# Attention, then a cosine MoE layer: raw w_out stores first, transposed probabilities in groups of six and eight, one PSUM copy shared by two engines

## The chip, the cores and the metric

The kernel runs on one core of one Trainium2 chip. The metric is the device time of one execution in microseconds. The profile follows the engines TensorE (PE, its weight loads PEld), VectorE (DVE), ScalarE (ACT), GpSimd (POOL) and SyncE (SP, which here only issues DMAs; a name with q is an engine's instruction queue).

## The reference

```python
# q, k, v: 4 batches, 12 heads, 448 positions, head width 64
scores = q @ k.T / sqrt(64);  scores[above the diagonal] = -1e9
attn = exp(scores - max);  attn = attn / (sum + 1e-9);  y = attn @ v
x = y as 1792 tokens x 768
h = x @ w_in            # 768 x 2048
out = (h * cos(h)) @ w_out   # 2048 x 768
```

The two weight matrices lie in DRAM as 64-bit floats; everything else is 32-bit.

## The kernel before

**Attention.** The work is 24 steps of one batch and two heads (`pairs`, N = 24). A step's rows are cut into seven blocks of 64 queries, and block m has m blocks of 64 keys. The instructions of each engine stand in the order in which the Python code writes them, so each engine is a queue. In step i (lines 596 to 626) PE computes the scores of pair i (`scores`, L391), the product with v of pair i-2 (`av`, L444), transposes q and k of pair i+2 (L341), transposes the probabilities of pair i-1 (`tp`, L424) and the finished output of pair i-2 (`turn_out`, L483). DVE adds the mask, takes each row's minimum and moves the scores from PSUM to SBUF in seven pieces (`masked`, L400), divides the output of pair i-2 (`divide`, L472 to L474), and copies transposed probabilities from PSUM to SBUF (L345). ACT makes the exponentials (L407) and the other copies from PSUM (L347, L502).

**The transposed probabilities.** They come in two groups (`GROUPS`), each for two heads, and each group and head fills one PSUM bank: `evac_tp(i, g, bs, h, dve)` copies one of these four from PSUM into the tile `pm`, on DVE where `dve` is true. Group 0 goes to banks 7 and 4, group 1 to banks 5 and 6. The same banks take the next step's scores: the first piece (m = 4) goes to bank 7, m = 7 to bank 4, m = 5, 1 and 2 to bank 6, m = 6 to bank 5. So the first scores of step i+1 wait for the copy of group 0, head 0, which is always DVE's first copy after the division. The copy of group 1, head 0 is DVE's when i is even and ACT's third when i is odd.

**The first weights.** Between steps, twelve pieces (128 x 256) of the first w_in and w_out tiles are turned into 32-bit floats (`convert_weight`), each piece in two halves. After an even step DVE shifts and masks the upper words (L139, L142); after an odd step it puts in the lower words (L148) and sets numbers below a bound to zero (L152). What POOL has to do for a piece is put into the list `postponed` and run at the start of the next step (`take_postponed`): after the first half the square of the upper word (L145), after the second the rounded high part and the rest (L156, L157). POOL also interleaves the raw q and k (L272) and splits the attention output into a high and a low part (L507, L508). A DMA that SP issues one step later stores the raw w_out piece (`raw_out`, L1427).

**The MoE part.** w_in and w_out are taken in 8 groups of 256 columns of the hidden layer. Every product is three matmuls: high x high, high x low, low x high. Tokens 0 to 1023 come first (`slot`), while DVE and ACT unpack the next weights (`mask`, `pack`), `halve` splits a tile (ACT L769, POOL L770) and POOL issues the DMAs that keep halves and raw w_out in DRAM (`spill_halves`, `spill_raw`). The other 768 tokens follow with seven block products in place of eight, from the tiles kept in DRAM.

Of the kernel before, what the change touches and what calls it, by code (L numbers as in the profile page):

```python
# [10 lines left out]
F32 = mybir.dt.float32  # L11
# [5 lines left out]
ALU = mybir.AluOpType  # L17
# [4 lines left out]
def kernel(  # L22
# [86 lines left out]
    def f32(ap):  # L109
        return ap.bitcast(F32)  # L110
# [20 lines left out]
    def convert_weight(st, w, pool, parts=1, j=0, halves=(0, 1)):  # L131
        n = DM // parts
        wh, wl = (w[:, x, j * n : (j + 1) * n] for x in range(2))
        lo32, hi32 = st[0][:, :, 0], st[0][:, :, 1]
        hif = f32(hi32)
        if 0 in halves:
            t = pool.tile([P, EH], U32, tag="ct", bufs=2, name="ct")[:, 0:n]
            st.append(t)
            nc.vector.tensor_scalar(  # L139
                t, hi32, 3, 0x3FFFFFFF, op0=ALU.logical_shift_left, op1=ALU.bitwise_and  # L140
            )
            nc.vector.scalar_tensor_tensor(  # L142
                t, hi32, 0xC0000000, t, op0=ALU.bitwise_and, op1=ALU.bitwise_or
            )
            return lambda: nc.gpsimd.tensor_tensor(hif, hif, hif, op=ALU.mult), None  # L145
        if 1 in halves:
            t = st[1]
            nc.vector.scalar_tensor_tensor(  # L148
                t, lo32, 29, t, op0=ALU.logical_shift_right, op1=ALU.bitwise_or
            )  # L150
            tf = f32(t)
            nc.vector.scalar_tensor_tensor(tf, hif, W_MIN2, tf, op0=ALU.is_ge, op1=ALU.mult)  # L152


            def rounded():
                nc.gpsimd.tensor_copy(wh, tf)  # L156
                nc.gpsimd.tensor_tensor(wl, tf, f32(wh), op=ALU.subtract)  # L157

            return rounded, tf
# [73 lines left out]
    def attention(filler_of, postponed):  # L233
        with (
# [108 lines left out]
            def evac(dst, src, dve=False):  # L343
                if dve:
                    nc.vector.tensor_copy(dst, src)  # L345
                else:
                    nc.scalar.copy(dst, src)  # L347
# [57 lines left out]
            def exps(i, *ms):  # L405
# [3 lines left out]
                    )  # L409

            GROUPS = [
                [(6, 0), (7, 0), (6, 1), (7, 1), (6, 2), (7, 2), (3, NM)],
                [(2, 0), (4, 0), (3, 0), (5, 0), (4, 1), (5, 1), (5, NM)],
            ]
            spots = {e: (g, x) for g, es in enumerate(GROUPS) for x, e in enumerate(es)}

            def open_ptr(i):
                ptr[i] = at.tile([P, 2, 2, NM, R], F32, tag="pm", bufs=2, name="pm")

            def tp(i, g, bs):  # L420
                for x, (m, kc) in enumerate(GROUPS[g]):
# [5 lines left out]
                        )  # L427

            def evac_tp(i, g, bs, h, dve=False):
                evac(  # L430
                    ptr[i][:, g, h].rearrange("p n r -> p (n r)"),
                    banks8[:, bs[h], 0 : NM * R], dve,
                )

            def obank(i):
                return 4 if i == N - 1 else 0

            def av(i):
                (vn, vo), pt, ob = vals.pop(i), ptr[i], obank(i)

                def add(m, j, y, lhsT, rhs, start=False, stop=False):
                    b, n, h = PLACE[m]
                    c = (2 * n + j) * E1
                    nc.tensor.matmul(  # L444
                        banks8[half(h), ob + b, c : c + E1], lhsT=lhsT, rhs=rhs, start=start, stop=stop
                    )

                for j in range(2):
                    for y in range(2):
                        for a, ms in enumerate(LAST):  # L450
                            m, ys = ms[y], half(y)
                            g, n = spots[ms[0], NM]
                            add(
                                m, j, y, pt[ys, g, j ^ SWAP[m], n],
                                vo[ys, a, i % 2, j] if y else vn[ys, m // 2, j], start=j == 0,
                            )
                pieces = [(7, 6, k) for k in range(3)] + [(5, 4, k) for k in range(2)] + [(2, 3, 0)]
                for x, (ma, mb, k) in enumerate(pieces):
                    for j in range(2):
                        for m in (ma, mb):  # L460
                            g, n = spots[m, k]
                            add(
                                m, j, 0, pt[:, g, j ^ SWAP[m], n], vn[:, k, j],
                                stop=j == 1 and x in (2, 5),
                            )

# [75 lines left out]
            for i in range(N):  # L542
                take_postponed()
                if i == 0:
                    load_raw(3)
                if i:
                    load_v(i)
                if i + 4 < N:
                    load_raw(i + 4)
                open_step(i)  # L550
                if i < 3:
                    scores(i, slice(0, 4))
                    if i < 2:
                        transpose_in(i + 1, TB_)
                    else:
                        tp(0, 1, (0, 1))
                    scores(i, slice(4, 8))
                if i == 0:
                    masked(i, 4, 3)
                    exps(i, 4)  # L560
                    evac_in(1, 0, True)
                    evac_in(1, 1)
                    masked(i, 7, 6, 5, 1, 2)
                    exps(i, 3, 7, 6, 5, 1, 2)
                    interleave(3)
                    yield i
                    continue
                if i == 1:
                    masked(i, 4, 3, 7, 6, 5)
                    evac_in(2, 0)  # L570
                    evac_in(2, 1)
                    exps(i, 4, 3)
                    open_ptr(0)
                    tp(0, 0, (0, 1))
                    evac_out(0, 0, (0, 1), 0)
                    masked(i, 1, 2)
                    exps(i, 7, 6)
                    interleave(4)
                    yield i
                    continue  # L580
                if i == 2:
                    transpose_in(3, TB_)
                    evac_out(0, 1, (0, 1), 0)
                    exps(1, 5, 1, 2)
                    masked(i, 4, 3)
                    exps(i, 4, 3)
                    masked(i, 7, 6)
                    exps(i, 7)
                    evac_in(3, 0, True)
                    evac_in(3, 1)  # L590
                    masked(i, 5, 1, 2)
                    exps(i, 6, 5, 1, 2)
                    av(0)
                    divide(0)
                    transpose_in(4, TB_)
                else:
                    scores(i)
                    if i < N - 1:
                        evac_in(i + 1, 0)
                        evac_in(i + 1, 1)  # L600
                    masked(i, 4, 3, 7, 6, 5, 1, 2)
                    exps(i, 4, 3, 7, 6, 5, 1, 2)
                    av(i - 2)
                    divide(i - 2)
                    if i < N - 2:
                        transpose_in(i + 2, TB_)
                G1, G2 = ((7, 4), (5, 6)) if i < N - 1 else (TB_, (4, 5))
                open_ptr(i - 1)
                tp(i - 1, 0, G1)
                evac_out(i - 1, 0, G1, 0)  # L610
                tp(i - 1, 1, G2)
                evac_tp(i - 1, 1, G2, 1)
                evac_tp(i - 1, 1, G2, 0, i % 2 == 0)
                if i == N - 1:
                    fill(4)
                if i + 3 < N:
                    interleave(i + 3)
                put_out(i - 2)
                if i == N - 1:
                    fill(2)  # L620
                    open_ptr(i)
                    tp(i, 1, (4, 5))
                    evac_out(i, 1, (4, 5), 0)
                    tp(i, 0, TB_)
                    evac_out(i, 0, TB_, 0)
                yield i
# [91 lines left out]
    def moe(ring, early, firsts):  # L718
        pend = None
        with tc.tile_pool(name="mo", bufs=1) as mo:  # L720
# [42 lines left out]
            def halve(i):  # L763
                if i >= len(todo):
                    return
                kind, f = todo[i]
                w = ring[kind, f] = weight_tiles(kind, (wpool, mo)[f // 2 % 2])
                tf = f32(masks.pop((i, 0))[:])
                nc.scalar.copy(w[:, 0], tf)  # L769
                nc.gpsimd.tensor_tensor(w[:, 1], tf, f32(w[:, 0]), op=ALU.subtract)  # L770
                spill_halves(kind, f, w)
                if kind:
                    spill_raw(f, tf)
                return tf

            def sums_tile(pool, tag, bufs, dtype=F32R):
# [714 lines left out]
```

## Time and profile before

| | |
|---|---|
| time, median of 3 runs | 592.44 us (591.93 to 592.61) |
| the profiled execution's own time | 589.68 us |
| its span in the profile | 587.9 us |
| busy share of the span | PE 99%, DVE 77%, ACT 68%, POOL 71% |
| chain that ended last, by engine | PE 81%, DVE 15%, issue 1%, DMA 1% |
| granted TensorE clock, mean | 0.998 |

PE is counted busy where its pipelined matmuls overlap, so its 99% doesn't say that it never waits. The chain that ended last is followed back from the last instruction: it says which engine's work set the end in each stretch. Its DVE share lies in the attention part; behind that it is PE almost alone.

### The profile page before, as it was taken

How to read it: one execution, taken by the hardware profiler on the slowest of the kernel's cores; microseconds unless marked ns; L12 is line 12 of the kernel's file. 1: busy time of each engine (PE TensorE's matmuls, PEld its weight loads, DVE VectorE, ACT ScalarE, POOL GpSimd, SP SyncE). 2: the span in 40 equal slices, each digit the busy share in tenths (PEclk: the TensorE clock that was granted, in tenths of full speed). 3: DMA queues.
4: the chain of work that ended last, by engine and by line, in shares of the span. 5: the costliest groups of instructions: out<-in, count | busy, mean ns of one | idle time of the engine just before them, and what ended most of it. 6: DMA issues, size and time to landing. Idle time of an engine off the chain costs nothing.

```text
span 587.9 us, 15297 instructions
## 1 busy us (share of the span) xinstructions
PE 579.7 (99%) x5895; PEld 538.9 (92%) x5895; DVE 455.2 (77%) x953; ACT 401.7 (68%) x788; POOL 419.6 (71%) x448
## 2 busy tenths in 40 slices
PE   9999999999999999999999999999999999999996
PEld 6888888888899999999999999999999999999996
DVE  5999999995767878778778767743587787787786
ACT  5999999997667777878777777532454554564540
POOL 2466666755377887977787877915678978978894
PEclk9999999999999999999999999999999999999999
DMA  9976676665268597876868796599987746748105
GB/s 182 211 175 156 163 177 156 167 178 184 80 216 299 171 337 257 300 273 210 303 197 313 218 337 225 229 354 401 378 293 246 255 160 231 263 164 284 43 1 161
DMA packets 92409, 131.55 MB, mean 224 GB/s; under 512 B 35024, under 2 KB 77216, under 8 KB 92336
## 3 DMA queue, kind: packets, MB, share of 16 engines
q1 hardware_dynamic: 84832, 106.52, 58.3%
q0 software_dynamic: 4736, 22.42, 9.9%
q10 hardware_dynamic: 2768, 1.64, 1.0%
q8 instruction: 46, 0.75, 0.5%
q14 instruction: 27, 0.22, 0.1%
HBM read 83.36 MB, written 47.19 MB: 222 GB/s over the span
## 4 chain that ended last, share of the span: by engine, by line
PE 81%; DVE 15%; DMA 1%; issue 1%; POOL 0%; ACTq 0%; DVEq 0%
PE banks L746 23%; PE banks L1175 13%; PE banks L1195 13%; PE banks L651 8%; PE banks L650 7%; PE banks L652 7%; DVE pb L400 7%; DVE pm L345 3%; PE banks L391 3%; DVE on L474 2%; PE banks L1212 2%; PE banks L1099 2%; PE banks L444 2%; DMA vn<-in_v_dram 1%; DVE ct L142 1%
## 5 line engine op out<-in xcount | busy, mean ns | idle before, releaser
L734 DVE TENSOR_TENSOR acc<-acc,banks 128x768 f32<-128x768 f32 (+1 forms) x122 | 112.7, 932 | 42.9 <-PE banks L746 32.6
L746 PE MATMUL banks<-w,gh 128*128 128x384 f32 x512 | 109.7, 335 | 0.0
L746 PEld LDWEIGHTS banks<-w,gh 128*128 128x128 f32 x512 | 90.9, 188 | 1.3 <-DVE acc L734 0.2
L651 PE MATMUL banks<-xa,w 128*128 128x512 f32 x192 | 75.2, 392 | 0.0
L652 PE MATMUL banks<-xa,w 128*128 128x512 f32 x192 | 75.0, 391 | 0.0
L650 PE MATMUL banks<-xa,w 128*128 128x512 f32 x192 | 74.9, 390 | 0.0
L407 ACT ACTIVATE pb<-pb,stat 128x256 f32<-128x256 f32 (+6 forms) x168 | 71.5, 527 | 2.6 <-DVE stat L400 2.6
L746 PE MATMUL banks<-w,gl 128*128 128x384 f32 x256 | 65.1, 335 | 0.0
L770 POOL TENSOR_TENSOR w<-ct,w 128x768 fp32r<-128x768 f32 x28 | 52.4, 1872 | 15.1 <-ACT w L769 9.1
L400 DVE CUSTOM_DVE_ANT_0 pb<-banks,mask 128x256 f32<-128x256 f32 (+6 forms) x168 | 60.1, 420 | 3.7 <-PE banks L391 3.7
L658 ACT ACTIVATE ni<-banks 128x512 int32<-128x512 f32 (+1 forms) x64 | 34.5, 539 | 33.7 <-PE banks L652 20.2
L677 POOL TENSOR_TENSOR gl<-r,gh 128x512 fp32r<-128x512 f32 x32 | 42.2, 1320 | 15.9 <-ACT gh L676 15.7
L660 DVE SCALAR_TENSOR_TENSOR r<-ni,banks 128x512 f32<-128x512 int32 (+1 forms) x56 | 35.1, 626 | 23.5 <-ACT ni L658 23.0
L662 ACT ACTIVATE r<-r 128x512 f32<-128x512 f32 (+1 forms) x56 | 32.8, 586 | 22.1 <-DVE r L660 21.5
L444 PE MATMUL banks<-vn,pm 128*64 128x65 f32 (+1 forms) x1344 | 47.5, 223 | 0.0
L746 PEld LDWEIGHTS banks<-w,gl 128*128 128x128 f32 x256 | 46.4, 188 | 0.0
L444 PEld LDWEIGHTS banks<-vn,pm 128*64 128x64 f32 (+1 forms) x1344 | 44.2, 137 | 1.8
L665 DVE SCALAR_TENSOR_TENSOR r<-r,banks 128x512 f32<-128x512 f32 (+1 forms) x56 | 35.0, 626 | 13.9 <-ACT r L663 13.9
L391 PE MATMUL banks<-flat 64*64 64x64 f32 (+5 forms) x768 | 43.5, 357 | 1.5 <-DVE pm L345 0.2
L1175 PE MATMUL banks<-xb,bb 128*128 128x384 f32 x234 | 44.7, 334 | 0.0
L652 PEld LDWEIGHTS banks<-xa,w 128*128 128x128 f32 x192 | 36.0, 188 | 7.5
L650 PEld LDWEIGHTS banks<-xa,w 128*128 128x128 f32 x192 | 36.1, 188 | 7.3
(143 smaller groups left out, 1430.5 us busy)
## 6 DMA issues: line engine op xcount, KB each, us to landing
bb<-w_in_d SPq DMA_DIRECT2D x48, 384.0 KB, 5.7
land<-in_moe_w_in_dram SPq DMA_DIRECT2D x14, 768.0 KB, 6.1
land<-in_moe_w_out_dram SPq DMA_DIRECT2D x14, 768.0 KB, 5.6
big<-w_out_d SPq DMA_DIRECT2D x25, 384.0 KB, 5.1
w_out_d<-w POOLq DMA_DIRECT2D x8, 768.0 KB, 5.1
w_in_d<-w POOLq DMA_DIRECT2D x7, 768.0 KB, 4.2
raw_d<-ct POOLq DMA_DIRECT2D x14, 384.0 KB, 6.5
vn<-in_v_dram SPq DMA_DIRECT2D x48, 96.0 KB, 4.0
```

The source lines that it names most:

```text
L391: nc.tensor.matmul(place(i, m)[heads(j ^ SWAP[m]), c : c + z - a], lhsT=qt[heads(j), (m - 1) * R : m * R], rhs=kt[heads(j), a:z], start=ba ...
L400: nc.vector.tensor_tensor_reduce(out=probs(i, m), in0=place(i, m), in1=mask[:, z : z + m * R], scale=-scale, scalar=3.0e38, op0=ALU.add, o ...
L407: nc.scalar.activation(probs(i, m), probs(i, m), AF.Exp, scale=-1.0, bias=stats[i][:, col(m)])
L444: nc.tensor.matmul(banks8[half(h), ob + b, c : c + E1], lhsT=lhsT, rhs=rhs, start=start, stop=stop)
L650: yield nc.tensor.matmul(hv, lhsT=wh[:, f], rhs=x[:, 0, cc, t], start=(cc == 0), stop=False)
L651: yield nc.tensor.matmul(hv, lhsT=wh[:, f], rhs=x[:, 1, cc, t], start=False, stop=False)
L652: yield nc.tensor.matmul(hv, lhsT=wl[:, f], rhs=x[:, 0, cc, t], start=False, stop=(cc == NCC - 1))
L734: nc.vector.tensor_tensor(d, d, o, op=ALU.subtract)
L746: nc.tensor.matmul(o[:, e, 0:EH], lhsT=a[:, cs], rhs=w[:, e * EH : (e + 1) * EH], start=(x == 0), stop=(x == 5),)
L770: nc.gpsimd.tensor_tensor(w[:, 1], tf, f32(w[:, 0]), op=ALU.subtract)
L1175: nc.tensor.matmul(o, lhsT=w[:, u, k * P : (k + 1) * P], rhs=x[k][:, v], start=k + m == 0, stop=k == K - 1 and m == 2,)
L1195: nc.tensor.matmul(o[:, b % 2, 0:EH], lhsT=g_ops[i][u][:, c * P : (c + 1) * P], rhs=wouts[g, i][:, v], start=(x == 0), stop=(x == 2),)
```

## The change

Four edits. (1) In `GROUPS` the piece (3, NM) goes from group 0 to group 1: the groups have six and eight blocks of 64 columns in place of seven and seven, so their copies have 384 and 512 columns, and `pm` is laid out by head. (2) The copy of group 1, head 0 becomes DVE's when i is odd; when i is even it is cut in two, 256 columns on ACT and 256 on DVE (`evac_shared`). (3) DVE's L152 goes: POOL makes the zero-or-one guard (a second instruction after the square) and multiplies with it (a first instruction ahead of the rounding). (4) In `halve` the raw w_out store is issued ahead of ACT's and POOL's work, not behind the store of the halves.

```diff
-            return lambda: nc.gpsimd.tensor_tensor(hif, hif, hif, op=ALU.mult), None
+            def guard():
+                nc.gpsimd.tensor_tensor(hif, hif, hif, op=ALU.mult)
+                nc.gpsimd.tensor_scalar(hif, hif, W_MIN2, None, op0=ALU.is_ge)
+            return guard, None
...
             tf = f32(t)
-            nc.vector.scalar_tensor_tensor(tf, hif, W_MIN2, tf, op0=ALU.is_ge, op1=ALU.mult)
             def rounded():
+                nc.gpsimd.tensor_tensor(tf, tf, hif, op=ALU.mult)
                 nc.gpsimd.tensor_copy(wh, tf)
                 nc.gpsimd.tensor_tensor(wl, tf, f32(wh), op=ALU.subtract)
...
             GROUPS = [
-                [(6, 0), (7, 0), (6, 1), (7, 1), (6, 2), (7, 2), (3, NM)],
-                [(2, 0), (4, 0), (3, 0), (5, 0), (4, 1), (5, 1), (5, NM)],
+                [(6, 0), (7, 0), (6, 1), (7, 1), (6, 2), (7, 2)],
+                [(3, NM), (2, 0), (4, 0), (3, 0), (5, 0), (4, 1), (5, 1), (5, NM)],
             ]
...
+            def evac_shared(i, b):
+                n, x = len(GROUPS[0]), len(GROUPS[1]) // 2
+                for y in range(2):
+                    evac(
+                        ptr[i][:, 0, n + y * x : n + (y + 1) * x].rearrange("p n r -> p (n r)"),
+                        banks8[:, b, y * x * R : (y + 1) * x * R], y == 1,
+                    )
...
-                evac_tp(i - 1, 1, G2, 0, i % 2 == 0)
+                if i % 2 or i > N - 2:
+                    evac_tp(i - 1, 1, G2, 0, i % 2 == 1)
+                else:
+                    evac_shared(i - 1, G2[0])
...
                 tf = f32(masks.pop((i, 0))[:])
+                if kind:
+                    spill_raw(f, tf)
                 nc.scalar.copy(w[:, 0], tf)
                 nc.gpsimd.tensor_tensor(w[:, 1], tf, f32(w[:, 0]), op=ALU.subtract)
                 spill_halves(kind, f, w)
-                if kind:
-                    spill_raw(f, tf)
```

In the changed kernel the line numbers move: DVE's copy L345 is L349, ACT's L347 is L351, L400 is L404, L472 to L474 are L486 to L488; on POOL L145 is L147, L156 and L157 are L160 and L161, L272 is L276, L507 and L508 are L521 and L522.

On DVE, the stretch between the division and the next masked scores, after an even step (first piece) and after an odd one (second piece). Before:

```order
L474 TENSOR_TENSOR on<-banks,r 128x512
L345 COPY pm<-banks 128x448 x2
L139 TENSOR_SCALAR ct<-st 128x256
L142 SCALAR_TENSOR_TENSOR ct<-st,ct 128x256
L400 ISA pb_147,stat<-banks,mask 128x256
...
L474 TENSOR_TENSOR on<-banks,r 128x512
L345 COPY pm<-banks 128x448
L148 SCALAR_TENSOR_TENSOR ct<-st,ct 128x256
L152 SCALAR_TENSOR_TENSOR ct<-st,ct 128x256
L400 ISA pb_145,stat<-banks,mask 128x256
```

The same two places on DVE in the changed kernel:

```order
L488 TENSOR_TENSOR on<-banks,r 128x512
L349 COPY pm<-banks 128x384
L349 COPY pm<-banks 128x256
L139 TENSOR_SCALAR ct<-st 128x256
L142 SCALAR_TENSOR_TENSOR ct<-st,ct 128x256
L404 ISA pb_147,stat<-banks,mask 128x256
...
L488 TENSOR_TENSOR on<-banks,r 128x512
L349 COPY pm<-banks 128x384
L349 COPY pm<-banks 128x512
L153 SCALAR_TENSOR_TENSOR ct<-st,ct 128x256
L404 ISA pb_145,stat<-banks,mask 128x256
```

The first copy has 64 columns less in both steps; the second has 192 less after an even step and is new after an odd one, where L152 is gone.

On POOL, one pair of steps, an even one and then an odd one, in the kernel before:

```order
L156 CAST w_487<-ct 128x256
L157 TENSOR_TENSOR w_487<-ct,w_487 128x256
L272 COPY land<-raw 128x896
L507 CAST xa<-xf 128x448
L508 TENSOR_TENSOR xa<-xf,xa 128x448
L145 TENSOR_TENSOR st<-st 128x256
L272 COPY land<-land 128x896
L507 CAST xa<-xf 128x448
L508 TENSOR_TENSOR xa<-xf,xa 128x448
```

And the same pair of steps on POOL in the changed kernel:

```order
L159 TENSOR_TENSOR ct<-ct,st 128x256
L160 CAST w_488<-ct 128x256
L161 TENSOR_TENSOR w_488<-ct,w_488 128x256
L276 COPY land<-raw 128x896
L521 CAST xa<-xf 128x448
L522 TENSOR_TENSOR xa<-xf,xa 128x448
L147 TENSOR_TENSOR st<-st 128x256
L148 TENSOR_SCALAR st<-st 128x256
L276 COPY land<-land 128x896
L521 CAST xa<-xf 128x448
L522 TENSOR_TENSOR xa<-xf,xa 128x448
```

Two instructions of 128 x 256 are new in each pair, and each stands ahead of an interleaving copy.

## Rows read from the trace of the kernel before

**Rows 1.** The span by stretches: us, then PE, PEld, DVE, ACT, POOL busy (instructions), clock, DMA, GB/s.

```profile
143.05:396.00 252.95, 252.95 (x1282) 230.33 (x1281) 187.38 (x232) 182.89 (x277) 188.69 (x174) 1.00 0.73 254
396.00:583.00 187.00, 186.79 (x1076) 186.08 (x1074) 141.61 (x218) 86.66 (x184) 148.55 (x147) 1.00 0.63 223
```

**Rows 2.** Timeline of PE, the scores of four steps: start, duration, engine, line, form.

```profile
20.32 1.83 PE L391 MATMUL banks<-flat 64*64 64x256 f32 x29
...
26.13 1.31 PE L391 MATMUL banks<-flat 64*64 64x256 f32 x20
...
58.37 1.75 PE L391 MATMUL banks<-flat 64*64 64x256 f32 x32
...
128.29 1.75 PE L391 MATMUL banks<-flat 64*64 64x256 f32 x32 [0.16 <-DVE pm L345]
```

**Rows 3.** Timeline of DVE, an even and an odd step; bracket: idle before, releaser.

```profile
52.33 1.15 DVE L345 COPY pm<-banks 128x448 f32<-128x448 f32 x2
53.39 0.28 DVE L139 TENSOR_SCALAR ct<-st 128x256 uint32<-128x256 uint32 x1
...
54.07 0.43 DVE L400 CUSTOM_DVE_ANT_0 pb<-banks,mask 128x256 f32<-128x256 f32 x1
...
57.70 0.61 DVE L345 COPY pm<-banks 128x448 f32<-128x448 f32 x1
58.23 0.41 DVE L148 SCALAR_TENSOR_TENSOR ct<-st,ct 128x256 uint32<-128x256 uint32 x1
58.75 0.43 DVE L152 SCALAR_TENSOR_TENSOR ct<-st,ct 128x256 f32<-128x256 f32 x1
59.44 0.42 DVE L400 CUSTOM_DVE_ANT_0 pb<-banks,mask 128x256 f32<-128x256 f32 x1 [0.27 <-PE banks L391]
...
62.02 0.17 DVE L472 TENSOR_SCALAR r<-banks 128x8 f32<-128x8 f32 x1
...
63.07 1.15 DVE L345 COPY pm<-banks 128x448 f32<-128x448 f32 x2
```

**Rows 4.** Waits of PE's weight loads, 26.13 to 128.3 us: total, times, longest.

```profile
PEld banks L391 <- DVE pm L345: 3.9, 19, 0.2
```

**Rows 5.** Groups of DVE's masked scores, 0 to 250 us: busy us, mean ns.

```profile
L400 DVE CUSTOM_DVE_ANT_0 pb<-banks,mask 128x448 f32<-128x448 f32 x24 | 14.9, 619 | 0.0
...
L400 DVE CUSTOM_DVE_ANT_0 pb<-banks,mask 128x384 f32<-128x384 f32 x24 | 13.3, 552 | 0.3 <-PE banks L391 0.3
```

**Rows 6.** Timeline of ACT, its copies of pm in an even and an odd step.

```profile
52.34 0.99 ACT L347 COPY pm<-banks 128x448 f32<-128x448 f32 x2
...
57.67 1.41 ACT L347 COPY pm<-banks 128x448 f32<-128x448 f32 x3
```

**Rows 7.** Timeline of POOL, an even step.

```profile
61.37 0.41 POOL L156 CAST w<-ct 128x256 fp32r<-128x256 f32 x1
61.86 0.74 POOL L157 TENSOR_TENSOR w<-ct,w 128x256 fp32r<-128x256 f32 x1
62.53 0.94 POOL L272 COPY land<-raw 128x896 f32<-128x896 f32 x1
64.64 0.66 POOL L507 CAST xa<-xf 128x448 fp32r<-128x448 f32 x1 [1.17 <-ACT xf L502]
```

**Rows 8.** Instructions of L142 and L152: shortest/median/longest ns, first and last start us.

```profile
L142 DVE SCALAR_TENSOR_TENSOR ct<-st,ct x12: 424/426/1065, 21.0 to 139.5; 128x256 uint32<-128x256 uint32 x12
...
L152 DVE SCALAR_TENSOR_TENSOR ct<-st,ct x12: 424/425/1190, 26.5 to 141.9; 128x256 f32<-128x256 f32 x12
```

**Rows 9.** Timeline of POOL beside the longest L142 and the longest L152.

```profile
20.89 0.94 POOL L272 COPY land<-raw 128x896 f32<-128x896 f32 x1 [2.87 <-DMA raw<-in_q_dram]
...
141.65 1.21 POOL L508 TENSOR_TENSOR xb<-xf,xb 128x448 fp32r<-128x448 f32 x1
```

**Rows 10.** Waits of SP, 85 to 146 us: total, times, longest.

```profile
SPq L1427 <- DVE ct L152: 11.8, 4, 8.9
```

**Rows 11.** The raw store's instructions on POOL: shortest/median/longest ns.

```profile
L221 POOL DMA_DIRECT2D raw_d<-ct x14: 547/552/662, 177.0 to 378.4; - x14
```

More of the change, by code (lines that the diff above doesn't have):

```diff
@@ L411, in attention @@
             GROUPS = [
-                [(6, 0), (7, 0), (6, 1), (7, 1), (6, 2), (7, 2), (3, NM)],
-                [(2, 0), (4, 0), (3, 0), (5, 0), (4, 1), (5, 1), (5, NM)],
+                [(6, 0), (7, 0), (6, 1), (7, 1), (6, 2), (7, 2)],
+                [(3, NM), (2, 0), (4, 0), (3, 0), (5, 0), (4, 1), (5, 1), (5, NM)],
             ]
-            spots = {e: (g, x) for g, es in enumerate(GROUPS) for x, e in enumerate(es)}
+            spots = {e: x for x, e in enumerate(GROUPS[0] + GROUPS[1])}
             def open_ptr(i):
-                ptr[i] = at.tile([P, 2, 2, NM, R], F32, tag="pm", bufs=2, name="pm")
+                ptr[i] = at.tile([P, 2, 2 * NM, R], F32, tag="pm", bufs=2, name="pm")
             def tp(i, g, bs):
@@ L429, in evac_tp @@
             def evac_tp(i, g, bs, h, dve=False):
+                n = len(GROUPS[0])
+                dst = ptr[i][:, h, n:] if g else ptr[i][:, h, :n]
                 evac(
-                    ptr[i][:, g, h].rearrange("p n r -> p (n r)"),
-                    banks8[:, bs[h], 0 : NM * R], dve,
-                )
+                    dst.rearrange("p n r -> p (n r)"),
+                    banks8[:, bs[h], 0 : len(GROUPS[g]) * R], dve,
+                )
+            def evac_shared(i, b):
[5 more added lines that the diff above has]
+                    )
             def obank(i):
@@ L451, in av @@
                             m, ys = ms[y], half(y)
-                            g, n = spots[ms[0], NM]
+                            n = spots[ms[0], NM]
                             add(
-                                m, j, y, pt[ys, g, j ^ SWAP[m], n],
+                                m, j, y, pt[ys, j ^ SWAP[m], n],
                                 vo[ys, a, i % 2, j] if y else vn[ys, m // 2, j], start=j == 0,
@@ L460, in av @@
                         for m in (ma, mb):
-                            g, n = spots[m, k]
+                            n = spots[m, k]
                             add(
-                                m, j, 0, pt[:, g, j ^ SWAP[m], n], vn[:, k, j],
+                                m, j, 0, pt[:, j ^ SWAP[m], n], vn[:, k, j],
                                 stop=j == 1 and x in (2, 5),
```

## Prediction

> **What bounds the kernel now.** I read the stretches first. From 143 us to the end of the MoE part PE's busy time equals the stretch to within 0.2 us [rows 1], so nothing that DVE, ACT, POOL or a queue gains there can shorten it; a gain has to arise before 143 us, and it then moves all that follows. So the next view is PE's timeline of the attention part. The scores of consecutive steps start 5.37 us apart: (58.37 - 26.13) / 6 = 5.373, and this holds for both kinds of step, from the start at 26.13 to that at 128.29 (19 intervals, 102.16 us, 5.377 each). Only the interval before, from 20.32, is longer: 5.81 [rows 2].
>
> The rows of DVE show what sets the 5.37. After the scores start at 58.37, the first masked piece follows at 59.44 (1.07 later, and DVE had waited 0.27 for PE). The seven pieces last until L472 at 62.02 (2.58), the division until the first copy of pm at 63.07 (1.05). That copy takes 0.61, and PE starts the next scores about 0.06 after it, at 63.74 [rows 2, 3]. 1.07 + 2.58 + 1.05 + 0.67 = 5.37: a closed loop of DVE and PE. PE waits in it: 19 waits of its score weights for DVE's copy, 3.9 us in all, 0.2 each [rows 4]. This 3.9 us is also the ceiling for anything that only frees PE earlier.
>
> What hangs on the loop but doesn't set it: behind the first copy DVE has other work before the next masked piece. In the even step that takes 52.33 to 54.07, 1.74 us; in the odd step DVE ends earlier and waits 0.27 [rows 3]. The path over PE, copy 0.61 + 0.06 + 1.07, is the same 1.74. So in even steps DVE's work and the scores end together, in odd steps the scores come last.
>
> **The change, part by part.** *First copy, 448 to 384 columns.* This is the one edit on the loop. The masked pieces of 448 and 384 columns, which DVE also reads from PSUM, differ by 619 - 552 = 67 ns [rows 5]. The starts at 20.32 and 128.29 have 20 intervals between them [rows 2]: 20 x 0.067 = 1.34 us.
>
> *Second copy and L152.* Does DVE keep up with the shorter path over PE, now 0.55 + 0.06 + 1.07 = 1.68? Even step: 0.53 per copy of 448 (53.39 - 52.33, halved) becomes 0.47 and, 192 columns less, 0.33; L139 and L142 need 0.68 (53.39 to 54.07) as before; 1.48 in all. Odd step: 0.47, then 0.60 for 512 columns, then L148 with at most 0.41: 1.48 [rows 3]. Both leave 0.2 us. So the removal of L152 (0.43 each, twelve times) gains nothing by itself in an odd step: it makes room for the second copy. Without that room the odd step would need 1.9 us and lose 0.2.
>
> *ACT.* A copy costs it 1.41 - 0.99 = 0.42. It has three pm copies in the odd step and two in the even one [rows 6]; now two and three, of 2048 columns in place of 2240 per two steps. The third is 256 wide, between 0.24 (in proportion) and 0.42. Its total falls, so I cost it at nothing; if the even step got late, the price is in the second rival.
>
> *POOL.* Neither new instruction is in the trace. Nearest are L156 (0.41) and L157, which takes 0.67 to the next start, and L272 with 0.94 [rows 7] bounds them from above. For the multiply I take 0.67, since L157 too has two inputs of 256 columns; for the guard 0.41 to 0.67. POOL has the room: it waits 1.17 for ACT in the even step. What matters is where L272 ends, because there is a collision to be had: L142 takes 424 to 426 ns, and once 1065; L152 takes 425, and once 1190 [rows 8]. The long ones lie beside L272, from 20.89, and L508, from 141.65 [rows 9]. So these two DVE instructions lose 0.6 to 0.8 us to a POOL instruction that is already running. In the even step L272 ends at 63.47, 0.27 before the scores start at 63.74. The multiply moves that by +0.67; the attention output reaches POOL some 0.35 earlier (ACT has one copy, 0.42, less ahead of it, and the wider one waits for two more transposes); the shorter step counts +0.07. So L272 ends 0.12 after the scores start, and L139 begins 0.19 after them (-0.61 + 0.80): no collision. With 0.41 or 0.94 for the multiply it ends at -0.14 or +0.39. L139, L142 and the masked piece need 0.68, and scores are ready at 1.07, so up to +0.39 even a collision costs nothing.
>
> *The first long interval.* At 21.0 L142 ran into L272, which had waited for its DMA until 20.89 [rows 8, 9]. It ended at 22.1, though the scores were ready at 20.32 + 1.07 = 21.39. In the changed kernel DVE reaches L142 some 0.2 earlier (copies 0.27 less, an earlier copy of group 1 with 0.07 more), at 20.83, just ahead of L272. If half-speed is what overlap means, the step wins about 0.3; I take 0.3. The Trainium skill ("SBUF — State Buffer", Who interferes with whom) says that it isn't a slowdown but a lock: a DVE instruction with two SBUF inputs and a GpSimd instruction share one port pair, whoever starts first has it, and the other blocks until the end. By that rule the step wins either 0.6 (L142 first, by 0.06 us) or nothing, and the sum would be 1.9 or 1.3.
>
> *Stores.* SP's raw store waits for POOL's multiply now, not for L152; it already waits up to 8.9 us there [rows 10]. Behind it stand v loads and the next weight piece, needed ten microseconds later: nothing. Issuing the raw store first in `halve` moves a POOL instruction of 0.55 us [rows 11] into the time in which POOL waits for ACT's copy; PE's unbroken work hides it [rows 1]. If that cover were gone, up to 0.55 for each of the 14 stores would be at stake, either way.
>
> Sum: 1.34 + 0.3 = 1.64 us, off 589.68 of the profiled execution: 588.0. The runs' median is 2.76 above the profiled execution, so 592.44 - 1.64 = 590.8.
>
> **The rivals.** *POOL runs into DVE in every even step: slower.* If the multiply takes 1.3 us in place of 0.67, L272 ends 0.77 after the scores start; then L139 and L142 follow and the masked piece starts at 1.45, not 1.07: +0.38 in ten even steps, 3.8 - 1.64 = 2.2 us slower, 594.6. It costs from +0.39 on, cancels the gain at +0.55, and makes the kernel measurably slower from about +0.67. For it: new instructions stand ahead of L272. Against: the nearest rows leave room. This is where the skill's lock would bite, L139 through L142 being the ones that wait.
>
> *Another wait takes over the loop: no change.* PE's wait is only 0.2 per step [rows 4], and ACT, with three copies in the even step, could give bank 4 back late: its first pm copy starts at 52.34, DVE's at 52.33 [rows 3, 6], so they end nearly together today. If ACT slips by 0.1, the 0.067 is gone and only the first interval may win: 592.1 to 592.4.
>
> *The gain is lost in the MoE part.* 440 us without a wait leave room for losses only: the new order of stores could let a buffer come free late. One or two stalls of 0.5 us: 591.5.
>
> **How the numbers follow.** Forecast (1.1 to 2.2 us faster) 0.67; a wait takes over 0.17; POOL collides 0.10; lost later 0.06. Two medians of this kernel can't be told apart below about 0.2%, 1.2 us. The forecast lies mostly above that, since both 1.3 and 1.9 do, but its lower end doesn't: faster 0.61. Slower needs the collision at full size: 0.08. The rest, 0.31, is no change. The forecast's own range is 590.2 to 591.4; the time that I give with 8 in 10 reaches from 589.9 to 592.5.
>
> **What would show it.** Right: scores 5.30 us apart in both kinds of step, PE's wait for the first copy still there but nearer 0.13 than 0.2; DVE waiting for PE ahead of the masked scores in even steps as well; L142 at 0.43 in all steps; PE without waits after 143 - 1.6 us. Wrong: L139 or L142 longer beside L276 in even steps (collision); score weights released by ACT's copy, not DVE's (a wait took over); an interval of 5.37 as before; waits of PE in the MoE part. The prediction would also fail if a first copy of 384 columns took as long as one of 448.

## The result: slower, 596.46 us

| | before | after |
|---|---|---|
| time, median (lowest to highest) | 592.53 us (591.92 to 593.82, 6 runs) | 596.46 us (595.25 to 597.69, 6 runs) |
| ratio to before, 95% interval | | 1.0079 [1.0062, 1.0096] |
| profiled execution, its span | 589.68, 587.9 us | 596.19, 594.4 us |
| start of the span to the fourth step's scores | 20.32 us | 22.02 us |
| fourth step's scores to the last step's | 107.97 us | 112.55 us |
| last step's scores to the end of the span | 459.61 us | 459.85 us |

The forecast was 590.8 and its range ended at 592.5. By the ratio the change costs 4.7 us, by the medians 3.9. The last three lines of the table divide the two profiled executions, whose spans differ by 6.5 us. 4.58 lie in the 20 steps of attention that the loop was worked out for, 0.24 in all that follows. The 1.70 ahead of the fourth step is no loss that can be put down to the change: there two traces of one kernel, "half first" below, are at 20.12 and 21.78. Two executions of the experiments below, one of 708.76 us at a granted clock of 0.75 and one of 1455.01 us, are left out of all medians and ratios; the first was its run's profiled one, so that run's row has no interval.

The first rows of after are the busy times by stretches (columns as in [rows 1]), and then the timeline of PE: start, duration, engine, line, form (compare [rows 2]).

```profile
143.05:396.00 252.95, 252.95 (x1375) 229.30 (x1372) 188.18 (x238) 186.56 (x284) 192.73 (x182) 1.00 0.74 251
```

```profile
22.02 0.80 PE L395 MATMUL banks<-flat 64*64 64x256 f32 x10
...
28.23 1.75 PE L395 MATMUL banks<-flat 64*64 64x256 f32 x32
...
50.83 1.75 PE L395 MATMUL banks<-flat 64*64 64x256 f32 x32
...
56.13 2.05 PE L395 MATMUL banks<-flat 64*64 64x256 f32 x29
...
62.13 1.75 PE L395 MATMUL banks<-flat 64*64 64x256 f32 x32
...
134.57 1.70 PE L395 MATMUL banks<-flat 64*64 64x256 f32 x27
```

PE has no idle time in the stretch of the MoE part, as before. In the attention part one interval is what I forecast (50.83 to 56.13, 5.30), the next is not (56.13 to 62.13, 6.00). All intervals of the first kind are 5.30 to 5.31 but for the last two, 5.36 and 5.39. Of the other kind, those of even steps, nine follow the long one at the start (22.02 to 28.23, 6.21): six of 5.99 to 6.00, and three of 5.73, between 90 and 118 us.

The even step in the timeline of DVE, ACT, POOL and PE; the bracket is the idle time before, and its releaser. The rows answer to [rows 3, 6, 7]; the last five stand for a later step, one of those with 5.73.

```profile
55.33 0.93 POOL L276 COPY land<-raw 128x896 f32<-128x896 f32 x1
55.44 1.31 ACT L351 COPY pm<-banks 128x384 f32<-128x384 f32 x3
55.53 0.55 DVE L349 COPY pm<-banks 128x384 f32<-128x384 f32 x1
56.13 2.05 PE L395 MATMUL banks<-flat 64*64 64x256 f32 x29
56.64 0.61 ACT L516 COPY xf<-banks 128x192 f32<-128x192 f32 x2
56.79 0.42 DVE L349 COPY pm<-banks 128x256 f32<-128x256 f32 x1 [0.71 <-ACT pm L351]
...
57.13 0.28 DVE L139 TENSOR_SCALAR ct<-st 128x256 uint32<-128x256 uint32 x1
57.32 0.56 POOL L521 CAST xa<-xf 128x448 fp32r<-128x448 f32 x1 [1.05 <-ACT xf L516]
57.45 0.71 DVE L142 SCALAR_TENSOR_TENSOR ct<-st,ct 128x256 uint32<-128x256 uint32 x1
...
58.08 0.41 DVE L404 CUSTOM_DVE_ANT_0 pb<-banks,mask 128x256 f32<-128x256 f32 x1
...
60.49 0.15 DVE L486 TENSOR_SCALAR r<-banks 128x8 f32<-128x8 f32 x1
...
90.03 2.05 PE L395 MATMUL banks<-flat 64*64 64x256 f32 x29
...
90.69 0.42 DVE L349 COPY pm<-banks 128x256 f32<-128x256 f32 x1 [0.71 <-ACT pm L351]
...
91.22 0.30 POOL L521 CAST xa<-xf 128x128 fp32r<-128x128 f32 x1 [1.05 <-ACT xf L516]
91.35 0.44 DVE L142 SCALAR_TENSOR_TENSOR ct<-st,ct 128x256 uint32<-128x256 uint32 x1
...
91.71 0.41 DVE L404 CUSTOM_DVE_ANT_0 pb<-banks,mask 128x256 f32<-128x256 f32 x1
```

DVE's first copy is as short as forecast, 0.55. Then DVE sits idle for 0.71, until ACT has finished the third of its copies (55.44 + 1.31 = 56.75): that third one is ACT's part of the bank that the two engines share. So L139 and L142 come late, and L142 now meets POOL's L521, which in an undisturbed step starts after it. L142 takes 0.71 there in place of 0.43. The first masked piece starts at 56.13 + 1.95 in place of + 1.07, and L486, the start of the division, at + 4.36; in the kernel before it was + 3.65 (58.37 to 62.02, [rows 2, 3]). The later step has the same wait of 0.71, but its L521 is short (0.30), L142 takes 0.44, and the masked piece starts at + 1.68.

The waits of DVE from 28 to 134 us (total, times, longest), and L142 and two of POOL's instructions (shortest/median/longest ns; compare [rows 8]):

```profile
DVE pm L349 <- ACT pm L351: 6.4, 9, 0.7
```

```profile
L142 DVE SCALAR_TENSOR_TENSOR ct<-st,ct x12: 430/704/712, 23.6 to 145.8; 128x256 uint32<-128x256 uint32 x12
...
L148 POOL TENSOR_SCALAR st<-st x12: 897/911/919, 25.9 to 147.0; 128x256 f32<-128x256 f32 x12
...
L159 POOL TENSOR_TENSOR ct<-ct,st x12: 735/748/760, 30.8 to 151.5; 128x256 f32<-128x256 f32 x12
```

Where the wait is in the program: the order of DVE's instructions in the built kernel, with what each waits for, around an even step.

```
L488 TENSOR_TENSOR on<-banks,r 128x512 [waits DVE_49]
L349 COPY pm<-banks 128x384 [waits PE_49]
L349 COPY pm<-banks 128x256 [waits PE_49,Activation_49]
L139 TENSOR_SCALAR ct<-st 128x256 [waits DMAHW2_49]
```

The two halves read different columns and write different parts of `pm`. They share only the PSUM bank, and the one whose code stands second, DVE's, waits for the other. That both write the tile `pm` is not the reason: in the kernel before, DVE's two copies at 52.33 and ACT's two at 52.34 write one `pm` from four banks, and no wait stands between them [rows 3, 6]. (The shared bank is bank 5. The next step's scores of m = 1 go there too, with m = 6, and not to bank 6 as the description of the kernel before has it.)

### The profile page after: what moved, and what is told of

It is laid out like the page before. It is cut to its first block, busy times and chain, and to the rows that moved or that the text cites. A ratio compares the mean times of both kernels' runs of the same rounds, so it can differ in the third digit from the quotient of the medians.

```text
span 594.4 us, 15325 instructions
## 1 busy us (share of the span) xinstructions
PE 586.6 (99%) x5895; PEld 541.6 (91%) x5895; DVE 454.3 (76%) x952; ACT 403.2 (68%) x788; POOL 439.1 (74%) x472
## 3 DMA queue, kind: packets, MB, share of 16 engines
q10 hardware_dynamic: 2768, 1.64, 1.0%
## 4 chain that ended last, share of the span: by engine, by line
PE 88%; ACT 6%; DVE 5%; issue 1%; ACTq 0%; DVEq 0%
PE banks L763 22%; PE banks L1192 13%; PE banks L1212 13%; PE banks L668 7%; PE banks L667 7%; PE banks L669 7%; PE banks L395 4%; PE banks L458 4%; ACT pb L411 3%; PE banks L1229 2%; PE banks L1116 2%; DVE pb L404 2%; ACT pm L351 2%; PE banks L428 2%; PE banks L345 2%
## 5 line engine op out<-in xcount | busy, mean ns | idle before, releaser
L404 DVE CUSTOM_DVE_ANT_0 pb<-banks,mask 128x256 f32<-128x256 f32 (+6 forms) x168 | 59.9, 417 | 3.7 <-PE banks L395 3.7
L395 PE MATMUL banks<-flat 64*64 64x64 f32 (+5 forms) x768 | 47.7, 363 | 0.1
L395 PEld LDWEIGHTS banks<-flat 64*64 64x64 f32 x768 | 33.4, 134 | 12.9 <-issue 2.4
L669 PEld LDWEIGHTS banks<-xa,w 128*128 128x128 f32 x192 | 36.0, 188 | 7.5
```

The source lines that it names most:

```text
L395: nc.tensor.matmul(place(i, m)[heads(j ^ SWAP[m]), c : c + z - a], lhsT=qt[heads(j), (m - 1) * R : m * R], rhs=kt[heads(j), a:z], start=ba ...
L404: nc.vector.tensor_tensor_reduce(out=probs(i, m), in0=place(i, m), in1=mask[:, z : z + m * R], scale=-scale, scalar=3.0e38, op0=ALU.add, o ...
L669: yield nc.tensor.matmul(hv, lhsT=wl[:, f], rhs=x[:, 0, cc, t], start=False, stop=(cc == NCC - 1))
```

## The experiments

Three theories. **W**: the loss is the wait of DVE's part of the shared copy for ACT's part, with what it brings in its train. **P**: POOL's longer list makes L139 or L142 late. **M**: the new order of the stores costs time in the MoE part. Every kernel was timed in the same job as the kernel before, which took 591.1 to 591.6 us there, about 1 us less than above; so the ratios count, and not the microseconds in the expectations. The last column is the time from the fourth step's scores to the last step's in its trace (before: 107.97).

| kernel | median, us | ratio to before | fourth to last scores, us |
|---|---|---|---|
| half first | 590.09 | 0.9986 [0.9972, 1.0000] | 106.74 |
| half first, again | 590.13 | 0.9980 [0.9962, 0.9999] | 106.63 |
| ACT's shared part first | 590.70 | 0.9986 [0.9974, 0.9999] | |
| ACT's shared part first, again | 591.01 | 0.9991 [0.9976, 1.0007] | 107.37 |
| third copy on ACT | 591.38 | 1.0006 [0.9995, 1.0017] | 107.85 |
| third copy on DVE | 591.08 | 1.0004 [0.9989, 1.0019] | 107.47 |
| store order only | 591.24 | 1.0006 [0.9991, 1.0021] | 108.08 |
| sharing only | 596.63 | 1.0084 [1.0068, 1.0100] | 113.18 |
| guard on POOL only | 593.55 | 1.0025 [0.9996, 1.0055] | 108.79 |
| groups only | 591.24 | 1.0000 [0.9985, 1.0015] | 109.07 |
| half first, guard on DVE | 594.15 | 1.0036 [1.0023, 1.0049] | 110.30 |

**Half first.** The changed kernel with the two halves issued in the other order, so that ACT's part waits for DVE's:

```diff
             def evac_shared(i, b):
-                for y in range(2):
+                for y in (1, 0):
```

> The changed kernel with DVE's half of the shared copy issued ahead of ACT's. Theory W (DVE's half waits in the program for ACT's half, and that late start makes the even steps 0.7 us longer): DVE no longer waits, scores start about 5.30 us apart in both kinds of step, 590.8 to 591.4 us, some 5 below the changed kernel. Theory P (POOL's longer list of work makes L139 and L142 late): the even steps stay near 6.0 and 5.7, 596 us. Theory M (the new order of the stores in the MoE part costs it): 596 us too, with waits of PE behind 145 us.

It was run again later, beside other kernels:

> The version with DVE's half issued first once more, beside the version above, since its first interval, 0.9972 to 1.0000, ended just at 1: W says 1.6 us less than before by the forecast's own sum, ratio 0.9965 to 1.0; P says 1.006 to 1.010, as the first run already ruled out. Intervals 5.30 in both kinds of step.

Timeline of the first of these runs, an even step:

```profile
51.42 0.93 POOL L276 COPY land<-raw 128x896 f32<-128x896 f32 x1
51.47 0.88 DVE L349 COPY pm<-banks 128x384 f32<-128x384 f32 x2
52.07 1.75 PE L395 MATMUL banks<-flat 64*64 64x256 f32 x31
52.27 0.28 DVE L139 TENSOR_SCALAR ct<-st 128x256 uint32<-128x256 uint32 x1
52.58 0.42 DVE L142 SCALAR_TENSOR_TENSOR ct<-st,ct 128x256 uint32<-128x256 uint32 x1
...
53.14 0.42 DVE L404 CUSTOM_DVE_ANT_0 pb<-banks,mask 128x256 f32<-128x256 f32 x1
53.32 0.56 POOL L521 CAST xa<-xf 128x448 fp32r<-128x448 f32 x1 [0.96 <-ACT xf L516]
```

The two copies of DVE follow each other, 0.88 together; L142 takes 424 to 426 ns in all twelve steps and ends before L521; the masked piece starts at + 1.07, and behind the first the intervals are 5.30 to 5.31 in both kinds of step, but for the last (5.39 in both runs) and one of 5.75 in the first run, which didn't come again in the second. POOL's list is here that of the changed kernel, so P falls as the cause. It does still meet DVE: in four even steps of the first run L139 runs into L276 and takes 0.48 to 0.65 (shortest/median/longest ns below), and the masked piece starts up to 0.16 late (+ 1.23), but those intervals are 5.30 too.

```profile
L139 DVE TENSOR_SCALAR ct<-st x12: 280/282/654, 20.3 to 137.7; 128x256 uint32<-128x256 uint32 x12
```

Against the changed kernel this order is worth 5.8 us in the trace (112.55 - 106.74), and both runs end below the kernel before, by 0.8 and 1.2 us; their intervals end at 1.0000 and 0.9999, so this small gain is only just told apart from none.

**ACT's shared part first.** Here all of the changed kernel stays, DVE's wait for ACT too; only ACT copies its 256 columns ahead of the 512 of the other head:

```diff
-                evac_tp(i - 1, 1, G2, 1)
                 if i % 2 or i > N - 2:
+                    evac_tp(i - 1, 1, G2, 1)
                     evac_tp(i - 1, 1, G2, 0, i % 2 == 1)
                 else:
                     evac_shared(i - 1, G2[0])
+                    evac_tp(i - 1, 1, G2, 1)
```

> The changed kernel with two copies of ScalarE exchanged in even steps: its 256 columns of the shared bank come ahead of the 512 of the other head. All else stays: the code order ACT's part, then DVE's part, the wait of DVE's part for ACT's, POOL's longer list, the stores. W: DVE's part still waits, but ACT is done with the bank about 0.5 earlier, so DVE's part starts at about scores + 0.15 in place of + 0.66, L139 and L142 end before POOL's L521 begins, the first masked piece comes at about scores + 1.25, the even intervals are 5.30 to 5.40 in place of 5.73 to 6.00, and the ratio to the kernel before is 0.998 to 1.0005. P: POOL's list is that of the changed kernel, so the ratio stays at 1.006 to 1.010.

The same kernel once more, for a trace of its intervals:

> The kernel of the run before last once more, for a trace at the full clock. W: DVE's part of the shared copy starts right behind ACT's part, at about scores + 0.2, L142 takes 0.43 in all steps and ends before POOL's L521 begins, even intervals 5.30 to 5.40, ratio 0.997 to 1.0005. P: even intervals 5.73 to 6.00 as in the changed kernel, ratio 1.006 to 1.010.

```profile
64.04 1.75 PE L395 MATMUL banks<-flat 64*64 64x256 f32 x32
64.17 0.42 DVE L349 COPY pm<-banks 128x256 f32<-128x256 f32 x1 [0.19 <-ACT pm L351]
...
64.83 0.42 DVE L142 SCALAR_TENSOR_TENSOR ct<-st,ct 128x256 uint32<-128x256 uint32 x1
...
65.17 0.42 DVE L404 CUSTOM_DVE_ANT_0 pb<-banks,mask 128x256 f32<-128x256 f32 x1
65.19 0.56 POOL L521 CAST xa<-xf 128x448 fp32r<-128x448 f32 x1 [0.90 <-ACT xf L516]
```

The wait is still there, 0.19 in place of 0.71. DVE's part starts at + 0.13, L142 ends before L521, and the masked piece comes at + 1.13: the interval is 5.31, as in all steps behind the first but four (5.52, 5.42, and the last two, 5.34 and 5.40). It is not the sharing as such that costs, and not that DVE waits, but that it waits behind two copies of ACT.

**Sharing only.** The kernel before, old groups, guard on DVE, old store order; the copy of group 1, head 0 is shared in even steps, four blocks to ACT and then three to DVE:

```diff
-                evac_tp(i - 1, 1, G2, 0, i % 2 == 0)
+                if i % 2:
+                    evac_tp(i - 1, 1, G2, 0)
+                else:
+                    evac_shared(i - 1, G2[0])
```

> The kernel before with one thing added: in even steps the copy of group 1, head 0 is shared, four blocks (256 columns) to ACT, then three (192) to DVE, in that order of code. No groups of six and eight, L152 stays on DVE, old store order. W (DVE's part waits for ACT's, since both read one bank): in even steps the first masked piece starts 0.6 to 0.9 later than scores + 1.07, even intervals 5.8 to 6.1, odd 5.37 as before: +0.45 to +0.7 in about ten steps, 4.5 to 7 us slower than before, ratio 1.008 to 1.012. P (POOL's longer list): POOL's list is the old one, so nothing is lost, ratio 0.999 to 1.001, intervals 5.37.

DVE's wait from 28 to 134 us, and the scores of three steps on PE:

```profile
DVE pm L345 <- ACT pm L347: 5.8, 9, 0.6
```

```profile
51.09 1.75 PE L391 MATMUL banks<-flat 64*64 64x256 f32 x32
56.47 1.91 PE L391 MATMUL banks<-flat 64*64 64x256 f32 x29
...
62.45 0.99 PE L391 MATMUL banks<-flat 64*64 64x256 f32 x14
```

5.38 and 5.98: the loss of the changed kernel is there in full (+ 5.2 us in the trace, + 5.0 by the ratio) with the sharing alone, as W said and P did not.

**Third copy on ACT, third copy on DVE.** The changed kernel without the sharing; the 512 columns of even steps go to ACT, or to DVE (then `evac_tp(i - 1, 1, G2, 0, True)` in every step):

```diff
-                if i % 2 or i > N - 2:
-                    evac_tp(i - 1, 1, G2, 0, i % 2 == 1)
-                else:
-                    evac_shared(i - 1, G2[0])
+                evac_tp(i - 1, 1, G2, 0, i % 2 == 1)
```

> The changed kernel with the copy of group 1, head 0 whole on ACT in even steps, nothing shared. Theory W: no copy reads the bank of another engine's copy, no wait; 590.8 to 591.6 us, if ACT, which then has 3 wide copies in even steps, is not late; DVE has 0.33 us less to do there. Theories P and M: about 596.

> The changed kernel with the copy of group 1, head 0 whole on DVE in every step, nothing shared. Theory W: no wait; DVE needs 0.46 + 0.60 + 0.68 = 1.74 us between its first copy and the masked scores in even steps, so about 5.37 there and 5.30 in odd steps: 591.5 to 592.2. Theory P: L142 begins 0.27 later than in a shared step without a wait, so it runs into POOL's L521 more often; 593 or more.

With the copy on ACT the even interval is mostly 5.40: L486 waits 0.17 to 0.18 for PE's product with v and starts at + 3.75 in place of + 3.66. That the product is late because ACT's third copy ends late fits the order of the two, but isn't shown. Two odd steps were longer (5.57, 5.52). With the copy on DVE it is 5.30 in both kinds of step. I had expected 5.37 there: 1.48 + 0.27 is more than the 1.68 of PE's path, but a masked piece that starts up to 0.17 late doesn't move L486, which waits for PE. Two steps of that run were longer: 5.52, and 5.57, where L142 ran into L521 and took 0.82, as P had it. Its first long interval was 6.13. The 20 steps gain 0.5 us in the trace (107.47), which the timing doesn't show (1.0004).

**Store order only.** The kernel before with the raw store ahead in `halve`, and nothing else.

> The kernel before with only the raw w_out store ahead of the halves. Theory W: nothing to gain or lose, 592.2 to 592.9 us. Theory M: most of the 4 us is here, 595 or more, with waits of PE behind 143 us.

The ratio's interval holds 1, behind the first the intervals are 5.37 to 5.38 but for three (5.42, 5.49 and the last, 5.46), and PE is busy without a gap from 143.05 to 396 us. M falls.

**Guard on POOL only.** The kernel before with L152 moved to POOL.

```diff
-            nc.vector.scalar_tensor_tensor(tf, hif, W_MIN2, tf, op0=ALU.is_ge, op1=ALU.mult)
...
+                nc.gpsimd.tensor_tensor(tf, tf, hif, op=ALU.mult)
```

> The kernel before with only the guard of the weights moved: is_ge and the multiply on POOL, L152 gone from DVE. W: POOL's longer list hits nothing, intervals 5.37 in both kinds of step, ratio 0.9985 to 1.001. P: in even steps POOL's weight-splitting or output instructions run beside L139 and L142, which take 0.7 and more in place of 0.43, even intervals 5.5 to 6.0: 1.5 to 6 us slower, ratio 1.0025 to 1.010.

The ratio is P's lowest, and its interval, from 0.9996 to 1.0055, reaches into W's range: the timing doesn't decide. The timeline has what P describes, in four even steps; two pieces of it, and the instructions of L139 (they took 281 to 284 ns in the kernel before):

```profile
55.30 0.56 POOL L511 CAST xa<-xf 128x448 fp32r<-128x448 f32 x1 [0.34 <-ACT xf L506]
55.31 0.82 DVE L142 SCALAR_TENSOR_TENSOR ct<-st,ct 128x256 uint32<-128x256 uint32 x1
...
97.77 1.75 PE L395 MATMUL banks<-flat 64*64 64x256 f32 x32
97.78 0.94 POOL L276 COPY land<-raw 128x896 f32<-128x896 f32 x1
...
98.17 0.70 DVE L139 TENSOR_SCALAR ct<-st 128x256 uint32<-128x256 uint32 x1
```

```profile
L139 DVE TENSOR_SCALAR ct<-st x12: 284/315/700, 22.4 to 141.7; 128x256 uint32<-128x256 uint32 x12
```

At 98.17 L139 runs into L276, which ends 0.95 after the scores start: my rival's collision at its place. The four steps are 0.1 to 0.4 longer each, 0.9 in all; a fifth long one (5.59) has no such meeting. So P's mechanism exists and is small. With half first the same meeting of L139 and L276 occurs but costs nothing.

**Groups only.** The kernel before with groups of six and eight; the assignment of copies, L152 and the stores as before.

> The kernel before with only the groups of six and eight: even steps two copies on DVE (384, 512), two on ACT; odd steps one on DVE (384), three on ACT; L152 on DVE, old store order. W (no bank is read by two engines): no wait between DVE and ACT; even steps 5.30, odd 5.30 to 5.40 (ACT's three copies end late there, as in the even steps with the third copy on ACT), so 0.0 to 0.07 per step less than before, 0.3 to 1.3 us faster, ratio 0.998 to 1.0. P says the same of this kernel, since POOL's list is the old one; it tells how much of the gain the grouping alone brings, against 0.9986 of the version with DVE's half first.

Behind the first two (7.15, 5.52) the intervals are 5.30 and 5.40, as expected; that is 0.02 per step less than 5.37, too little for the timing, which gives 1.0000. The trace's 109.07 holds one stall that no other trace has, in the chain that ended last:

```profile
27.40 1.22 issue
```

**Half first, guard on DVE.** The first version with only the third edit undone: L152 is back on DVE (L153 here).

> The version with DVE's half first, but with the guard back on DVE (L152), so only the third edit is undone there. My step on the second copy said that without the room that L152 leaves an odd step needs 1.9 in place of 1.68 and loses 0.2. W with the loop as the later traces show it (the first masked piece may be 0.17 late before the division is): masked pieces at scores + 1.25 to 1.35 in odd steps, odd intervals 5.30 to 5.42, even 5.30: 0 to 1.2 us slower than with the guard on POOL, ratio 0.998 to 1.001. P: POOL's list is the old one, so this is the fastest of all, ratio below 0.9986.

```profile
61.00 1.75 PE L391 MATMUL banks<-flat 64*64 64x256 f32 x32
...
61.46 0.42 DVE L149 SCALAR_TENSOR_TENSOR ct<-st,ct 128x256 uint32<-128x256 uint32 x1
...
61.95 0.56 POOL L517 CAST xa<-xf 128x448 fp32r<-128x448 f32 x1 [1.78 <-ACT xf L512]
61.98 0.80 DVE L153 SCALAR_TENSOR_TENSOR ct<-st,ct 128x256 f32<-128x256 f32 x1
...
62.71 0.41 DVE L400 CUSTOM_DVE_ANT_0 pb<-banks,mask 128x256 f32<-128x256 f32 x1
```

Both expectations missed: it is slower than the kernel before (1.0036), and by 3.6 us in the trace than with the guard on POOL (110.30 - 106.74). Behind the longer second copy L153 comes just after POOL's L517 has begun, takes 0.80 in place of 0.43, and the masked piece starts at + 1.71, not at + 1.30. Odd intervals are 5.75, and 5.48 where L517 is split in a short and a longer one; the first is 6.02, the last 5.85.

## Why the prediction was wrong

**The loop and the first copy: right.** 5.37 less 0.067 is 5.30, the interval of the undisturbed steps, in the changed kernel and in each experiment with groups of six and eight. The first copy took 0.55 in place of 0.61. In the changed kernel all odd steps up to 118 us have it. The sign that I named is there too: with half first PE's weight loads for the scores start 0.14 after the ones before them end (51.60 + 0.33 to 52.07), where they waited 0.20 before [rows 4] and I had put 0.13.

```profile
51.60 0.33 PEld L497 LDWEIGHTS banks<-ident,on 64*128 64x128 f32 x7
52.07 0.32 PEld L395 LDWEIGHTS banks<-flat 64*64 64x64 f32 x12
```

One link I misread: I let the seven masked pieces last until the division. They take 2.41 where they start late (+ 1.95 to + 4.36), against 2.58 from 59.44 to 62.02 in the kernel before; the rest, 0.17, is a wait for PE's product with v, so a late masked piece has that much more room than I allowed.

**Second copy, even step: this step failed.** I wrote 0.47 + 0.33 + 0.68 = 1.48 against 1.68 of PE's path, "both leave 0.2 us". The durations were right: with half first the four instructions take 1.45 (51.47 to 52.92, 0.08 before L142's end, as L404 starts in the changed kernel). What failed is the premise that the second copy follows the first at once. (My term for ACT failed with it: "Its total falls, so I cost it at nothing". Not its total counts, but when its third copy ends, 0.62 after the scores start.) It waits for ACT's third copy and starts at + 0.66 in place of about - 0.14: 0.80 late, and L142 loses 0.28 to POOL's L521. 0.80 + 0.28 - 0.20 of slack = 0.88, the masked piece's delay (1.95 - 1.07). Of that 0.17 is hidden behind PE's product with v, so L486 is 0.70 late, and 5.30 + 0.70 is the 6.00 of the rows. In the three steps with the short L521 it is 1.68 - 1.07 - 0.17 = 0.44, for an interval of 5.73. Six times 0.70 and three times 0.43 are 5.5; the first interval is 0.77 above that of the version with half first, which makes 6.3. The two traces differ by 5.8, since one step of that version was 0.45 longer.

The wait stood in the order of the built program, which I had read without the waits. The Trainium skill states it too ("PSUM — Partial Sum Buffer", PSUM bank collisions raise a hardware error): two engines must not touch one bank in the same partitions at the same time, two readers included, and a dependency between them is what keeps them apart. The order and the 0.71 agree with the dependency; what happens without it, no run here shows. I had read the shared copy as two independent halves.

**None of my rivals was this one.** The collision that I priced at 594.6 was with L276 at L139. In the changed kernel L276 ends 0.13 after the scores start (55.33 + 0.93), as forecast with 0.12, and L139 takes 0.28. The collision that came, L142 with L521, followed from the wait. The rival itself is real in the kernel with the guard alone on POOL, but my threshold for it was too low. With half first L276 ends up to 0.68 after the scores start (94.70 + 0.93, scores at 94.95) and costs nothing, where I had a cost from 0.39 on: L139 ends 0.15 after L276 instead of taking its full 0.28, and the 0.17 above comes on top. (Its sum was off as well: a multiply of 1.3 lets L276 end at + 0.75, not + 0.77, so 594.4.) POOL's guard took 0.91, above the 0.41 to 0.67 that I gave it, and the multiply 0.75 in place of 0.67; neither is on the path. That another wait takes over was a rival, but on ACT's bank 4 and at no change.

**L152: half right.** I said that its removal makes room for the second copy, and that without it an odd step loses 0.2. The direction holds; the size was 0.45 in early odd steps and 0.18 in late ones, since L152 would meet POOL there.

**First interval: right in kind, not in size.** I took 0.3, which rested on half speed; the lock, which the traces show (last section), gave 0.6 or nothing. In the two runs with half first L142 doesn't meet L276, and the interval is 5.44 and 5.71, in place of 5.81: 0.37 and 0.10 are won, and the masked piece waits 0.2 to 0.3 for PE there; where L276, which waits for its DMA, started just ahead of L142, it is longer than before (6.09 with ACT's shared part first, L142 1.03). When the load lands differs from run to run, so this is luck and not a term to count on.

**Stores, MoE part: right.** No effect that can be measured.

Over the 20 steps the version with half first comes near the sum, 1.23 and 1.34 us less than before where I had 1.64. By the ratios it is 0.8 to 1.2 us below the kernel before, only just clear of noise, and some 5.5 to 5.9 below the changed one, far clear of it.

## What to carry to other kernels

Before one PSUM bank is divided between two engines, ask which of the two is made to wait, and what stands ahead of the other's part on its engine: let the engine on the critical path go first, by the order of the code, or let the other engine do the shared part first of all. Read the waits of the built order, not only the instructions. And a delay in a tightly packed schedule costs more than itself: a copy that starts 0.80 late became 1.08 of delay here, because the late instruction met one of POOL's that it had always been ahead of.

## What the runs showed of the hardware

DVE's two-input instructions on SBUF that start while a POOL instruction runs end a fixed time after it, 0.27 to 0.28 in every such meeting of the traces, however long both are: L142 0.27 after L521 in the changed kernel (57.45 + 0.71 against 57.32 + 0.56, and 91.35 + 0.44 against 91.22 + 0.30, to 0.01), and 0.27 in the kernel with the guard on POOL (55.31 + 0.82 against 55.30 + 0.56); L153 0.27 after L517 (61.98 + 0.80 against 61.95 + 0.56). That is a wait until POOL ends, not a lower speed, as the Trainium skill has it ("SBUF — State Buffer", Who interferes with whom). L139, with one input, did the same in the kernel with the guard on POOL: 0.70 in place of 0.28, its end 0.15 after L276's (98.17 + 0.70 against 97.78 + 0.94).

Some traces have a step that was 0.2 to 0.45 longer with no wait for another engine that would account for it. In the kernel with ACT's shared part first it was a gap of 0.25 on DVE between L486 and L487:

```profile
51.97 0.20 DVE L487 RECIPROCAL r<-r 128x8 f32<-128x8 f32 x1 [0.25 <-DVE r L486]
```

It stands in the same step, the ninth, with the third copy on DVE (52.04), with the third copy on ACT (51.66) and in the kernel with the guard on POOL (53.09), but in neither run with half first. The 5.75 of half first is another pause, 0.58 in PE's weight loads of the eleventh step. Their causes stay open.
